# Loading two x tiles and half of the scale weights on a second DMA queue in a transformer block

## Chip, cores and metric

The kernel runs on one core of one Trainium2 chip. The metric is device time in microseconds (us), lower is better. The engines that the text names are TensorE (PE in the profile; PEld is its weight load), VectorE (DVE), ScalarE (ACT), GpSimd (POOL) and SyncE (SP). SyncE and ScalarE can both issue DMAs; each does it in its own instruction order and has its own queue (SPq and ACTq in the profile are instructions of their sequencers). The chip's 16 DMA engines move the data.

## The reference

A block with conditional layer norm (adaLN), linear attention and a gated feed-forward part, on S = 2048 rows of width D = 1024, all in bf16:

```python
mod = (silu(c) @ w_mod).reshape(...)              # sa, ca, ga, sb, cb, gb: six rows of 1024
h = layernorm(x) * (1 + ca) + sa
qkv = h @ wqkv                                     # 32 heads of 32
pq, pk = phi(q), phi(k)                            # phi(t) = where(t > 0, t + 1, exp(t)) + 1e-6
o = (pq @ (pk^T v)) / (pq . sum(pk) + 1e-6)        # per head, no softmax
x = x + ga * (o @ wo)
h = layernorm(x) * (1 + cb) + sb
x = x + gb * ((silu(h @ w_gate) * (h @ w_up)) @ w_down)   # F = 3584
```

For the change, what matters is the beginning: the scale `1 + ca` multiplies the normalized x before the first projection, so both x and the part of `w_mod` that gives `ca` (1024 x 1024) have to be on chip first.

## The kernel before

Rows are tiled by 128 (16 row tiles, "st") and by chunks of 512 (4 chunks of 4 tiles). A small planner in the file (`_Prog`) takes instructions in the order in which the code names them, puts each on its engine's list, and finds the waits from the memory that each reads and writes. It doesn't reorder: every engine, and SyncE with its DMAs, works its list from top to bottom. All instructions are recorded by one helper, so that nearly all lines of the profile have the line L176, and instructions are told apart by the names of their tiles. `P.dma` (line 192) puts a load on SyncE's list unless `queue` says otherwise. Each load has a semaphore of its own ("lane").

The work begins with the first chunk:

- Loads (lines 397 to 430): `c` (2 KB) on the ScalarE queue; then on the SyncE queue, in this order, the row tiles 0 to 3 of x (`x0_0` to `x0_3`, 256 KB each, tile XRES), `wca0` (1 MB, the first 512 columns of the scale weights, tile WCA), `wq0` (512 KB, the rows 0 to 255 of the q weights, tile WQK), `wca1` (1 MB), `wq2`, `wq4` (512 KB each), `wsa1` (1 MB, half of the shift weights), `wq6`, `wq7`, `wsa0`, then x tiles of the second chunk, the k weights, and x tiles of the third.
- TensorE transposes c, ScalarE computes silu(c) (SILUC; its function table has to be loaded first), VectorE copies it to fp32 (SILUF). TensorE fills its time with 13 dummy matmuls on a zero tile (`warm`, tiles e and ident).
- Statistics (from line 617): tile 1 on ScalarE (`act_stats`, out tile ht as a scratch), tiles 0, 2, 3 on VectorE (`bn_stats`). VectorE's order is: SILUF, statistics of tile 0, statistics of tile 2, then the factors that ScalarE needs to normalize tile 0 (`nmr`). ScalarE normalizes tiles 0 and 1, VectorE 2 and 3.
- TensorE's order then is: transposes of tile 0, 5 dummy matmuls, transposes of tile 2, `mod_sc(WCA, 8, range(2))` (16 matmuls of one column, which compute the first quarter of ca and wait for wca0), transposes of tiles 1 and 3, `mod_sc(WCA, 8, range(2, 4))`, and the first 14 matmuls of the q projection (`q_part` in `q_phase_chunk0`, line 742), which need the scaled h (`h0_first`, VectorE) and wq0. After these come `mod_sc(WCA, 8, range(4, 8))`, which waits for wca1, and the q projection with wq2, wq4 and so on.

After this start the kernel goes on through the k and q projections of all chunks, the attention products, the output projection and the feed-forward part, with TensorE at work nearly all the time.

Of the kernel before, what the change touches and what calls it, by code (L numbers as in the profile page):

```python
# [262 lines left out]
def bass_adaLN_cond__linear_attn_block__swiglu_ffn__prompt_kernel(  # L263
# [12 lines left out]
    S, D = A_x.shape[1], A_x.shape[2]  # L276
# [9 lines left out]
    with ExitStack() as es:  # L286
# [6 lines left out]
        def T(name, off, shape, dt):  # L293
            n = 1
            for s_ in shape[1:]:
                n *= s_
            assert off % 32 == 0 and off + n * mybir.dt.size(dt) <= ARENA, (name, off, shape)
            return nc.alloc_sbuf_tensor_at(name, shape, dt, offset=base + off)

        KB = 1024  # L300
        XRES = T("xres", 0, [128, NST, D], BF16)
        PQT = T("pqt", 32 * KB, [128, NHG, S], BF16)
        WCA = T("wca", 32 * KB, [128, NDT, D], BF16)
# [81 lines left out]
        xv = A_x[0].rearrange("(t p) d -> p t d", p=128)  # L385
# [6 lines left out]
        wmv = w_mod.rearrange("(kt p) n -> p kt n", p=128)  # L392
        cv8 = c.rearrange("o (kt p) -> (o kt) p", p=128)

        P = _Prog()

        P.dma("c", CS8[0:NDT, :], cv8, queue="act")
        for st in range(4):
            P.dma("x0_%d" % st, XRES[:, st, :], xv[:, st, :])

        def ca_load(p):
            P.dma("wca%d" % p, WCA[:, :, 512 * p:512 * p + 512], wmv[:, :, D + 512 * p:D + 512 * p + 512])

        def sa_load(p):
            P.dma("wsa%d" % p, WSA[:, :, 512 * p:512 * p + 512], wmv[:, :, 512 * p:512 * p + 512])
# [1 line left out]
        def wq_load(i, n=1):  # L407
            P.dma("wq%d" % i, WQK[:, i:i + n, 0:D], wqkvv[:, i:i + n, 0:D])

        ca_load(0)  # L410
        wq_load(0, 2)
        ca_load(1)
        wq_load(2, 2)
        wq_load(4, 2)
# [684 lines left out]
        for ch in range(NCH):  # L1099
# [39 lines left out]
            for j in range(4):  # L1139
                st = 4 * ch + j  # L1140
# [62 lines left out]
```

## Time and profile before

| | us |
|---|---|
| median of 3 runs (lowest to highest) | 831.15 (830.88 to 831.25) |
| the profiled execution, whole time | 831.22 |
| its span, first to last instruction | 829.4 |
| TensorE busy | 824.0 (99%) |
| VectorE busy | 312.0 (38%) |
| ScalarE busy | 197.6 (24%) |
| DMA, mean over the span | 144 GB/s |
| first transposes on TensorE (start) | 8.76 |
| first matmuls on wca0 (start) | 10.74 |
| first matmuls of the q projection (start) | 12.43 |

Times in the profile are from the start of the span. A line of the timeline gives start, duration, engine, line, operation, tiles (out<-in), shapes and count, and in square brackets the idle time before it and what ended that. For a DMA, the duration is that of its issue in the sequencer; the time from issue to landing is shown apart. A line of a wait gives who waited, for whom, the sum in us, how often, and the longest.

### The profile page before, as it was taken

The page shows a single profiled execution, that of the slowest core. Times are in us where ns is not written, and L with a number is a line of the kernel's source. Part 1 is how long each engine was busy: PE and PEld are TensorE (multiplying, and loading weights), DVE is VectorE, ACT ScalarE, POOL GpSimd, SP SyncE. Part 2 cuts the span into 40 slices and gives each one's busy share as a digit, 9 for nine tenths or more (in the row PEclk, how much of TensorE's full clock was granted, in tenths as well). Part 3 has the DMA queues.
Part 4 walks back from the last instruction along what each step waited for, and adds up shares of the span by engine and source line. Part 5 has one row for each costly group of instructions (what it writes and reads, how often), then busy time and mean ns, then how long its engine had stood idle before and what let it go on. Part 6 is the DMA issues. An engine that isn't in the chain of part 4 may idle for free.

```text
span 829.4 us, 10017 instructions
## 1 busy us (share of the span) xinstructions
PE 824.0 (99%) x4083; PEld 378.4 (46%) x4083; DVE 312.0 (38%) x665; ACT 197.6 (24%) x336; POOL 39.8 (5%) x57
## 2 busy tenths in 40 slices
PE   8999999999999999999999999999999999999998
PEld 4544444454444444444444444444444444444444
DVE  5797986756955521121221111122111111221111
ACT  4757641323242111011111101111110111111011
POOL 1010000000130000030000003000000300000000
PEclk9999999999999999999999999999999999999999
DMA  9969655928397996700455570045557004553000
GB/s 320 288 151 229 149 159 172 202 102 304 60 258 225 259 267 174 192 25 14 128 150 155 150 188 28 15 126 153 153 153 187 26 18 125 154 151 86 0 26 26
DMA packets 199245, 119.28 MB, mean 144 GB/s; under 512 B 57880, under 2 KB 182944, under 8 KB 199200
## 3 DMA queue, kind: packets, MB, share of 16 engines
q1 hardware_dynamic: 199184, 118.65, 52.7%
q8 instruction: 32, 0.52, 0.3%
q14 instruction: 13, 0.11, 0.0%
q10 hardware_dynamic: 16, 0.00, 0.0%
HBM read 100.67 MB, written 4.33 MB: 127 GB/s over the span
## 4 chain that ended last, share of the span: by engine, by line
PE 99%; DMA 1%; DVE 0%; ACT 0%; SPq 0%; issue 0%
PE ps L176 99%; DMA xres<-in_A_x_dram 1%; DVE stats L176 0%; ACT xres L176 0%; SPq L176 0%; DVE xres L176 0%; DVE mv L176 0%; DVE nmr L176 0%
## 5 line engine op out<-in xcount | busy, mean ns | idle before, releaser
L176 PE MATMUL ps<-h2t,gug 128*128 128x512 bf16 x896 | 211.7, 379 | 0.0
L176 PE MATMUL ps<-h2t,guu 128*128 128x512 bf16 x896 | 211.7, 379 | 0.0
L176 DVE TENSOR_TENSOR at<-sg,ps 128x512 bf16<-128x512 bf16 x112 | 77.1, 688 | 282.7 <-PE ps L176 281.1
L176 ACT ACTIVATE sg<-ps 128x512 bf16<-128x512 f32 x112 | 66.9, 597 | 309.7 <-PE ps L176 309.7
L176 PEld LDWEIGHTS ps<-h2t,guu 128*128 128x128 bf16 x896 | 87.5, 98 | 105.8
L176 PEld LDWEIGHTS ps<-h2t,gug 128*128 128x128 bf16 x896 | 87.4, 98 | 105.7
L176 PE MATMUL ps<-wd_a,at 128*128 128x512 bf16 (+1 forms) x512 | 112.4, 378 | 0.0
L176 PE MATMUL ps<-ht,wqk 128*128 128x512 bf16 x512 | 111.7, 379 | 0.0
L176 PE MATMUL ps<-wd_b,at 128*128 128x512 bf16 (+1 forms) x384 | 85.0, 378 | 0.0
L176 PEld LDWEIGHTS ps<-wd_a,at 128*128 128x128 bf16 x512 | 50.0, 98 | 59.8
L176 DVE TENSOR_TENSOR ut<-att,gb_b 128x512 bf16<-128x512 bf16 (+1 forms) x32 | 13.8, 430 | 167.5 <-ACT att L176 167.5
L176 PEld LDWEIGHTS ps<-ht,wqk 128*128 128x128 bf16 x512 | 49.4, 98 | 58.8
L176 ACT ACTIVATE att<-ps 128x512 bf16<-128x512 f32 (+1 forms) x32 | 17.4, 591 | 182.1 <-PE ps L176 182.1
L176 PEld LDWEIGHTS ps<-wd_b,at 128*128 128x128 bf16 x384 | 37.5, 98 | 44.7
L176 PE MATMUL ps<-pk,xres 128*128 128x512 bf16 x256 | 56.5, 379 | 0.0
L176 PE MATMUL ps<-mw,pqt 128*128 128x512 bf16 x256 | 56.3, 379 | 0.0
L176 POOL TENSOR_SCALAR h2t<-h2t,modcol 128x512 bf16<-128x512 bf16 x32 | 26.4, 841 | 383.0 <-DMA h2t<-xn 383.0
L176 ACT ACTIVATE e<-ps 128x512 bf16<-128x512 f32 x56 | 33.1, 603 | 31.7 <-PE ps L176 20.5
L176 PEld LDWEIGHTS ps<-mw,pqt 128*128 128x128 bf16 x256 | 24.8, 98 | 30.3 <-DVE xres L176 0.4
L176 PEld LDWEIGHTS ps<-pk,xres 128*128 128x128 bf16 x256 | 24.8, 98 | 30.0 <-issue 0.4
L176 ACT ACTIVATE junk<-xres 128x1024 bf16<-128x1024 bf16 x24 | 25.4, 1058 | 35.1 <-DVE xres L176 34.9
L176 DVE SCALAR_TENSOR_TENSOR xres<-ps,xres 128x512 bf16<-128x512 f32 x32 | 21.4, 689 | 12.3 <-PE ps L176 11.7
(107 smaller groups left out, 346.0 us busy)
## 6 DMA issues: line engine op xcount, KB each, us to landing
gug<-in_B_w_gate_dram SPq DMA_DIRECT2D x56, 512.0 KB, 3.9
guu<-in_B_w_up_dram SPq DMA_DIRECT2D x56, 512.0 KB, 5.2
xres<-in_A_x_dram SPq DMA_DIRECT2D x20, 256.0 KB, 7.8
rb<-recip_den SPq DMA_DIRECT2D x8, 512.0 KB, 11.5
stgx<-in_w_mod_dram SPq DMA_DIRECT2D x2, 2048.0 KB, 7.8
wd_a<-in_B_w_down_dram SPq DMA_DIRECT2D x4, 1024.0 KB, 7.8
out_dram<-xres SPq DMA_DIRECT2D x31, 128.0 KB, 1.7
xres<-in_A_x_dram SPq DMA_DIRECT2D x3, 1024.0 KB, 14.0
```

Source lines behind the costliest of these rows:

```text
L176: return getattr(e, method)(**kw)
```

## The change

The row tiles 1 and 3 of the first chunk are issued on the ScalarE queue instead of the SyncE queue, and so is the first half of the scale weights. On ScalarE's list these three issues stand behind the load of c and ahead of the load of the function table for silu(c). On SyncE's list the order becomes x0_0, x0_2, wq0, wca1, wq2, and so on as before. The lists of TensorE, VectorE and GpSimd are the same.

```diff
         P.dma("c", CS8[0:NDT, :], cv8, queue="act")
         for st in range(4):
-            P.dma("x0_%d" % st, XRES[:, st, :], xv[:, st, :])
+            P.dma("x0_%d" % st, XRES[:, st, :], xv[:, st, :], queue="act" if st % 2 else "sp")
 
         def ca_load(p):
-            P.dma("wca%d" % p, WCA[:, :, 512 * p:512 * p + 512], wmv[:, :, D + 512 * p:D + 512 * p + 512])
+            P.dma("wca%d" % p, WCA[:, :, 512 * p:512 * p + 512], wmv[:, :, D + 512 * p:D + 512 * p + 512],
+                  queue="act" if p == 0 else "sp")
```

## Prediction

> **What bounds the kernel now.** I read the chain that ended last first, in order of time, because it tells which wait the end hangs on.
>
> ```profile
> 1.71 4.21 DMA xres<-in_A_x_dram
> ...
> 5.94 1.29 DVE stats L176 x2
> ...
> 7.47 1.23 ACT xres L176
> ...
> 8.76 818.08 PE ps L176 x4069
> ```
>
> From 8.76 us on, TensorE alone carries the chain, for 818.08 us. What stands before it is the start: row tile 2 of x lands at 5.92, VectorE takes its statistics, ScalarE normalizes tile 0, and the first transposes run. So a microsecond is won or lost only in front of 8.76, or where TensorE is made to wait after it. The second view is the waits of TensorE over the whole span.
>
> ```profile
> PE ps L176 <- DMA cs<-in_c_dram: 2.2, 1, 2.2
> PE ps L176 <- ACT xres L176: 0.4, 1, 0.4
> PE ps L176 <- DVE e L176: 0.2, 1, 0.2
> ```
>
> All three lie before 8.8 us. After that no wait is listed, so nothing later can swallow a delay: what the start loses, the end loses. The third view is TensorE's timeline around the first use of the weights that the change moves (start, duration, instruction).
>
> ```profile
> 8.76 0.62 PE L176 MATMUL ps<-ident,xres 128*128 128x128 bf16 x8 [0.42 <-ACT xres L176]
> 9.21 1.24 PE L176 MATMUL ps<-e,ident 128*128 128x512 bf16 x5
> 10.29 0.61 PE L176 MATMUL ps<-ident,xres 128*128 128x128 bf16 x8
> 10.74 0.54 PE L176 MATMUL ps<-siluc,wca 128*128 128x1 bf16 x16
> 11.14 1.05 PE L176 MATMUL ps<-ident,xres 128*128 128x128 bf16 x16
> 12.03 0.54 PE L176 MATMUL ps<-siluc,wca 128*128 128x1 bf16 x16
> 12.43 3.18 PE L176 MATMUL ps<-ht,wqk 128*128 128x512 bf16 x14
> ```
>
> The scale matmuls at 10.74 read WCA's first half (wca0). Behind them in TensorE's order stand the other transposes and the first projection matmuls (12.43), which need the scale. When did wca0 land? The fourth view is the wca loads singly (issue time, then time from issue to landing), the first for half 0, the second for half 1.
>
> ```profile
> L176 SPq DMA_DIRECT2D wca<-in_w_mod_dram x1: 434/434/434, 2.6 to 2.6; - x1
> ...
> DMA to landing us min/median/max: 7.8/7.8/7.8
> ```
> ```profile
> L176 SPq DMA_DIRECT2D wca<-in_w_mod_dram x1: 479/479/479, 3.8 to 3.8; - x1
> ...
> DMA to landing us min/median/max: 11.0/11.0/11.0
> ```
>
> Half 0, issued at 2.65, landed at 10.4, only 0.3 us before its use at 10.74. Half 1, issued at 3.80, landed at 14.8. The same view of the other loads gives x tiles at 3.6, 4.2, 5.9 and 6.6, wq0 (issued 3.12, 8.7 later) at 11.8, and wq2 (4.32, 11.8 later) at 16.1. They land in the order of issue, with 1 MB of x by 6.6, 2 MB by 10.4, 2.5 MB by 11.8, 3.5 MB by 14.8, 4 MB by 16.1. The last view, of stretches of 3 us, says why (last two columns: DMA share, GB/s).
>
> ```profile
> 1.80:4.80 3.00, 2.38 (x7) 0.91 (x8) 1.92 (x8) 1.59 (x3) 0.00 (x0) 1.00 0.90 274
> 4.80:7.80 3.00, 3.00 (x9) 0.97 (x7) 2.29 (x9) 2.11 (x5) 0.57 (x1) 1.00 1.01 348
> 7.80:10.80 3.00, 2.58 (x26) 1.44 (x25) 2.83 (x8) 1.90 (x2) 1.26 (x2) 1.00 1.08 380
> 10.80:13.80 3.00, 3.00 (x57) 2.29 (x55) 2.28 (x7) 1.79 (x3) 0.00 (x0) 1.00 1.09 362
> ```
>
> The DMA engines are full from 1.8 us on. The issue of a 256 KB tile takes 0.40 to 0.43 us on SyncE, far less than the 0.7 us that 256 KB takes at 360 GB/s. The start is short of DMA bandwidth, not of issue time.
>
> **What the Trainium skill says.** "DMA: Bandwidth & Descriptors", section "Issuing engines are not separate DMA queues": DMAs from different engines end up on the same 16 DMA engines and interleave, so a second issuer saves only sequencer time. The trace of before has only one tiny load on the ScalarE queue (2 KB, c), so it can't show the interleaving, but the full DMA share fits the rest. Same page, "Queues, rings and completion order": each DMA engine goes round between the queue rows that have work, one packet at a time. No run so far shows that; it is what I build on. "ScalarE activation tables: per-element evaluation and per-set limits" gives a table load as 1283 ns; the first one here is 1.28 us, from 1.40, straight after the c load.
>
> **The change part by part.**
>
> (a) Order among the transfers, on the path. Before, one queue gave x0, x1, x2, x3, wca0, wq0, wca1, wq2. After, SyncE's queue holds x0, x2, wq0, wca1, wq2 and so on, ScalarE's holds x1, x3, wca0. Nothing is added or removed in bytes. But wca0 no longer stands ahead of wq0 and wca1: it shares with them. ScalarE's queue carries 1.5 MB; with equal bytes to each queue SyncE's gets 1.5 MB through as well, plus a lead, since x1 can be issued on ScalarE only behind c (0.78 to 1.36) where x0 goes at 0.79: 0.57 us at 274 GB/s is 0.15 MB. So wca0 ends with 3.15 MB through in place of 2 MB. In the landings of before 2.5 MB stand at 11.8 and 3.5 MB at 14.8, so 3.15 MB is 11.8 + 0.65 x 3.0 = 13.75 us. That is 3.0 us after the use at 10.74. Bounds: if the turns are packet by packet, wca0's 1 KB rows meet wq0's 2 KB rows and lose some: SyncE gets 0.17 MB more, 3.3 MB, 14.2. Below, the bytes moved in the last view come to 0.82 + 1.04 + 1.14 = 3.0 MB by 10.8, so 3.15 MB (3.3 million bytes) are through at 10.8 + 0.3/0.362 = 11.6, landed by about 11.9. That differs by 1.8 us from the landings, which follow the slowest of the engines; if that one lags less after the change, 11.9 is right. I take 13.75 since the lag is there in the one trace. TensorE starts the scale matmuls about 0.05 after the landing: 13.8 - 10.74 = +3.06 us.
>
> (b) What else is late then. Behind wca0 the spacing on TensorE stays (10.74 to 12.43), as statistics, transposes of tile 2 and the x tiles are done by then. wq0 comes earlier (two turns after x). wca1 and wq2 keep their places at 3.5 and 4 MB, 14.8 and 16.1; their uses were at 15.45 and 16.25 and move to 18.5 and 19.3. So no second stall, and no gain. The later loads (wsa, x tiles 4 on) keep their bytes ahead of them and their landing; TensorE asks for them 3 us later.
>
> (c) ScalarE: three DMA issues now stand before its table load. One costs 0.43 (SyncE's row) to 0.58 us (c on ScalarE): 1.3 to 1.75 us. The table load goes from 1.40 to 2.7 to 3.1, silu(c) ends at 4.2 to 4.6, and VectorE's copy of it, which stands ahead of the first statistics in VectorE's order, ends at 4.4 to 4.85. The statistics of tile 0 began at 3.64, so +0.75 to +1.2; those of tile 2 waited for their data until 5.94 and could have begun at 5.38 otherwise (VectorE's timeline has the last step before them from 5.21, 0.15 long), so 0.56 of this is absorbed: +0.2 to +0.65 on the first transposes, 8.76 to about 9.1. I take +0.35. It is hidden wholly in the 3.06 of (a), since TensorE waits at the scale matmuls anyway; if wca0 comes in time, it is the whole cost.
>
> (d) Arrival of x. Tile 2 is second in its queue now, but shares with tiles 1 and 3: it ends with about 0.8 MB through, near 6.1, against 5.92. Tile 1 near 4.9, tile 3 near 6.9 against 4.2 and 6.6; ScalarE's statistics of tile 1 would start at 4.9 in place of 4.27, beside (c). At zero, under (a).
>
> (e) SyncE: three issues fewer (0.41 + 0.43 + 0.43 = 1.27 us). Its later loads are issued earlier, yet the issue of wq2 already took 3.9 us in a full queue. Zero; this is what (a) uses against wca0.
>
> Sum: +3.06 us on the profiled execution's 831.22 (span 829.4, 1.8 around it), 834.3. The median of the runs is 831.15, 0.07 lower, so 834.2.
>
> **The rivals.**
> R1, the lag goes: wca0 lands at 11.9, +1.2 us, 832.4. For it: the bytes moved. Against: the landings of before.
> R2, wca0 in time, not slower: if the engines don't share evenly, but ScalarE's short queue drains ahead (large turns), wca0 has 1.5 MB of its own and about 0.5 to 0.7 MB of the other ahead, and lands by 10.4 to 11. Then only (c) is left, +0.2 to +0.65 with tile 2 at its time of before: 831.5. It decides when wca0 lands before about 11.1 (10.74 and that 0.35). Against: SyncE's queue is never empty then. That this becomes a gain is excluded: VectorE can't begin before 4.4 and needs 1.74 us from its first statistics to those of tile 2 (3.64 to 5.38) and 2.82 from there to the transposes (5.94 to 8.76), so 8.96 at the earliest, after 8.76.
> R3, SyncE's queue is favoured: wca0 comes behind all of wca1, at 14.8 or later, up to 16: +4.1 to +5.3, 835.9.
>
> **How the numbers follow.** Forecast (landing 12.8 to 14.3) 0.60; R1 0.22; R2 0.12; R3 0.06. The range leaves R2 and R3 out: 831.8 to 835.2. What a measurement of this kernel can tell from no change is about 0.2%, 1.66 us: slower is above 832.8. Forecast and R3 are slower, and about a third of R1 (0.08): 0.74. The rest of R1 and R2, but for 0.02, are the same: 0.24. Faster by 1.66 us has no mechanism that I see, so 0.02 for what I don't see.
>
> **What would show it.** In the profile after, the chain must get a DMA of wca in it, TensorE must have a wait for wca of about 2.5 to 3 us ending near 13.8, and the first projection matmuls must start near 15.5. wq0 must land at 9 to 10.3. The table load must start at 2.7 to 3.1. The stretch from the first projection to the end must keep its length. It would be wrong if wca0 landed by 11.1, or if the chain still ran through the tile-2 statistics.

## The result: 5.6 us slower

| | before | after |
|---|---|---|
| median of 6 runs each, us (lowest to highest) | 831.07 (830.88 to 831.25) | 836.66 (835.79 to 837.82) |
| the profiled execution, us | 831.22 | 837.27 |
| its span, us | 829.4 | 835.5 |
| first transposes on TensorE (start) | 8.76 | 8.80 |
| first scale matmuls, on wca0 (start): S | 10.74 | 14.53 |
| third group of scale matmuls, on wca1 (start) | 15.45 | 21.53 |
| from the first group to the third: L | 4.71 | 7.00 |

S and L are read from the profiled execution, the medians from all. The ratio of the medians is 1.0068, with a 95% interval of 1.0055 to 1.0081. The forecast was 834.2 with a range of 831.8 to 835.2: slower, as measured, but by too little.

The chain that ended last, of the kernel after (start, duration, what):

```profile
2.30 12.18 DMA wca<-in_w_mod_dram
14.48 0.05 issue
14.53 818.38 PE ps L176 x4048
```

The tile-2 statistics are gone from the chain. wca0 is in it instead, 12.18 us from its issue to its landing at 14.48, and then TensorE to the end. The three longest of TensorE's waits over the whole span, after:

```profile
PE ps L176 <- DMA wca<-in_w_mod_dram: 3.4, 1, 3.4
PE ps L176 <- DMA cs<-in_c_dram: 2.2, 1, 2.2
PE ps L176 <- ACT xres L176: 1.4, 1, 1.4
```

The first line is new. So far this is the forecast. TensorE's timeline after, around the wait, shows what is not:

```profile
8.80 0.62 PE L176 MATMUL ps<-ident,xres 128*128 128x128 bf16 x8 [1.40 <-ACT xres L176]
...
10.55 0.62 PE L176 MATMUL ps<-ident,xres 128*128 128x128 bf16 x8
14.53 0.58 PE L176 MATMUL ps<-siluc,wca 128*128 128x1 bf16 x16 [3.35 <-DMA wca<-in_w_mod_dram]
14.97 1.87 PE L176 MATMUL ps<-ident,xres 128*128 128x128 bf16 x16
16.63 0.61 PE L176 MATMUL ps<-siluc,wca 128*128 128x1 bf16 x16
17.11 4.58 PE L176 MATMUL ps<-ht,wqk 128*128 128x512 bf16 x14
21.53 0.94 PE L176 MATMUL ps<-siluc,wca 128*128 128x1 bf16 x32
```

The scale matmuls start 3.79 us later than before. But the 16 transposes behind them take 1.87 us (1.05 before), and the 14 projection matmuls, 17.11 to 21.53, take 4.42 us where 12.43 to 15.45 were 3.02 before. The same instructions run at little over half their rate until about 20. Nothing waits there. The stretches of 2 us of the kernel after say why (the third column from the right is the granted TensorE clock):

```profile
10.00:12.00 2.00, 1.12 (x11) 0.45 (x9) 1.04 (x3) 1.24 (x1) 0.56 (x1) 1.00 1.10 349
12.00:14.00 2.00, 0.00 (x0) 0.00 (x0) 0.00 (x0) 0.00 (x0) 0.00 (x0) 0.79 1.09 367
14.00:16.00 2.00, 1.47 (x27) 1.48 (x28) 0.48 (x2) 0.00 (x0) 0.00 (x0) 0.50 1.05 379
16.00:18.00 2.00, 2.00 (x27) 1.45 (x26) 1.78 (x6) 1.10 (x2) 0.00 (x0) 0.50 1.10 352
18.00:20.00 2.00, 2.00 (x6) 0.67 (x5) 0.41 (x2) 1.41 (x2) 0.00 (x0) 0.51 1.07 368
20.00:22.00 2.00, 2.00 (x27) 1.16 (x26) 0.00 (x0) 0.00 (x0) 0.00 (x0) 1.00 1.08 358
```

While TensorE sat idle its clock was halved, and it got the full clock back only at 20. A mean of 0.79 over 12 to 14 is 0.84 us at half, so the fall was at about 13.2. The account of this execution is then whole: S + 3.79 for the wait, L + 2.29 for the clock, 6.08 us, against 6.1 us between the spans.

The mean granted clock is on record for every execution. With 3.4 us at half in 835 us it would be 0.998, with 6.8 us (13.2 to 20.0 above) 0.996. Of the six executions of the kernel after, the three with 0.998 took 835.79 to 836.33, the three with 0.996 took 837.00 to 837.82, and none kept 1.000. So the loss goes with the clock from one execution to the next, and the median of 836.66 lies between the two groups.

The Trainium skill has this in "TensorE: Matmul & The Clock Gate", Part 1 (the clock gate): TensorE's clock falls to a half after an idle window of about 3.4 us and rises again after a busy window of that length, and the windows run freely. The traces agree with the half clock and with the length: it lasts 6.8 us here, twice 3.4. They don't agree with a whole idle window: the clock fell at 13.2, 2 us after TensorE's last work at 11.2. The last section has more on this.

### The profile page after: what moved, and what is told of

The parts are those of the page before. It is cut to its first block, busy times and chain, and to the rows that moved or that the text cites. A ratio compares the mean times of both kernels' runs of the same rounds, so it can differ in the third digit from the quotient of the medians.

```text
span 835.5 us, 10017 instructions
## 1 busy us (share of the span) xinstructions
PE 825.7 (99%) x4083; PEld 380.1 (45%) x4083; DVE 312.3 (37%) x665; ACT 197.6 (24%) x336; POOL 39.9 (5%) x57
## 4 chain that ended last, share of the span: by engine, by line
PE 98%; DMA 1%; ACTq 0%; DVE 0%; issue 0%
PE ps L176 98%; DMA wca<-in_w_mod_dram 1%; ACTq L176 0%; DVE xres L176 0%
```

## The experiments

**My theory** after the result: wca0's packets take turns with the other queue's, which makes it late and TensorE wait; and the idle time costs the clock, so that the time is S (wait) plus L (clock). **Rival A**: the three DMA issues on ScalarE, ahead of its table load, delay the start. **Rival B**: the clock is a by-product, and the whole loss is the wait for data. **Rival C**: two queues at once move less than one.

In every row S, L and the span are of one profiled execution, and medians and ratios are of all executions of the run; S and L are read from TensorE's timeline as above, and "sum" is (S - 10.74) + (L - 4.71). The span difference is against 829.4. In e2, e3 and e6 the clock was low ahead of S already, so there S too holds a part of the clock's cost. In e10 the sum leaves 0.3 us open; a wait of 0.2 us on VectorE elsewhere is listed there and not before.

| run | S | L | sum | span difference | median, us | before, same chip | ratio (95% interval) |
|---|---|---|---|---|---|---|---|
| e1_x_only | 11.07 | 4.75 | 0.37 | 0.4 | 832.03 | 831.53 | 1.0011 (1.0003 to 1.0020) |
| e2_wca_only | 14.58 | 5.22 | 4.35 | 4.4 | 834.28 | 831.53 | 1.0024 (1.0013 to 1.0035) |
| e3_after_fill | 16.01 | 4.72 | 5.28 | 5.3 | 835.35 | 831.53 | 1.0047 (1.0032 to 1.0062) |
| e4_one_queue_late | 15.06 | 7.58 | 7.19 | 7.2 | 837.83 | 831.53 | 1.0075 (1.0060 to 1.0090) |
| e5_late_fill | 14.80 | 4.73 | 4.08 | 4.1 | 834.43 | 831.22 | 1.0040 (1.0025 to 1.0055) |
| e6_no_warm | 12.22 | 5.09 | 1.86 | 1.9 | 832.83 | 831.22 | 1.0020 (1.0011 to 1.0028) |
| e7_wq_act | 11.29 | 4.76 | 0.60 | 0.6 | 831.98 | 831.22 | 1.0009 (1.0002 to 1.0016) |
| e8_wca_split | 11.47 | 4.73 | 0.75 | 0.7 | 832.00 | 831.22 | 1.0008 (0.9999 to 1.0017) |
| e9_after_fill2 | 14.33 | 4.73 | 3.61 | 3.6 | 834.93 | 831.37 | 1.0050 (1.0036 to 1.0063) |
| e10_sp_2k | 15.21 | 7.24 | 7.00 | 7.3 | 838.45 | 831.37 | 1.0082 (1.0069 to 1.0095) |
| e11_after | 13.70 | 7.57 | 5.82 | 5.9 | 836.89 | 831.37 | 1.0061 (1.0048 to 1.0074) |

### Which part of the change does it

**e1**, wca0 put back on SyncE's queue:

```diff
-            P.dma("wca%d" % p, WCA[...], wmv[...],
-                  queue="act" if p == 0 else "sp")
+            P.dma("wca%d" % p, WCA[...], wmv[...])
```

> Only the two x tiles go on the ScalarE queue; wca0 is back on the SyncE queue. Theory (wca0's place among the packets makes TensorE wait about 3.8 us, and the wait lets the clock fall to half for a while, about 2.3 us more): wca0 lands at 10.4 to 10.8, no wait for it over 0.3 us, clock 1.0 throughout, 831.1 to 831.6 us. Rival A (the issues on ScalarE, ahead of its table load, delay the start): two of the three issues stay, so most of the loss stays, 834 us or more.

832.03, 0.5 us over the kernel before and 0.4 over the top of my range. wca0 landed at 8.9, earlier than I had said, and L is 4.75: no clock lost in the profiled execution. Two of the three issues on ScalarE stayed, and nearly all of the loss was gone, so rival A falls. Two of the twelve executions did lose the clock (mean 0.998) and took 834.42 and 834.53. The 0.4 us of the profiled execution are the x tiles: tile 3 landed at 8.2 (6.6 before), its statistics on VectorE began at 8.27 (7.88), and tile 2, which VectorE normalizes behind them, was transposed from 10.61 (10.29).

**e2**, wca0 alone on ScalarE's queue:

```diff
-            P.dma("x0_%d" % st, XRES[:, st, :], xv[:, st, :], queue="act" if st % 2 else "sp")
+            P.dma("x0_%d" % st, XRES[:, st, :], xv[:, st, :])
```

> Only wca0 goes on the ScalarE queue; the four x tiles stay on SyncE. Theory: wca0 alternates with wq0 and wca1 and lands near 13.5 to 14.5, TensorE waits over 2.5 us for it, the clock falls, 835.5 to 837.8 us. Rival A (issues on ScalarE): one issue of the three, 831.5 to 833 us.

My theory missed here. 834.28, less than expected, and by another way. The median hides three groups: three of the eight executions kept the clock (mean 1.000) and took 832.41 to 832.56, only 1.0 us over the kernel before; four with 0.998 took 834.20 to 834.70; and the profiled one, with 0.996, was the slowest, 835.58. The kernel is the same in all three. In the profiled execution wca0, issued right behind c at 1.40, landed at 10.3, in good time. What came late were the x tiles 2 and 3, at 7.9 and 9.1. TensorE's longest wait in e2 is the normalized tile, not wca:

```profile
PE ps L176 <- ACT xres L176: 3.6, 1, 3.6
```

and the DMA queues between 4 and 5 us (q1 is SyncE's, q10 ScalarE's; packets, MB, share of 16 engines) show who had the engines:

```profile
q10 hardware_dynamic: 255, 0.26, 77.2%
q1 hardware_dynamic: 23, 0.05, 14.1%
```

The rule is the same (what stands at the head of the second queue competes with what is urgent in the first), the victim another. The idle time cost the clock here too: the 5 dummy matmuls behind the first transposes took 2.34 us, against 1.24 before.

**e7**, wq0 on ScalarE's queue in place of wca0:

```diff
-                  queue="act" if p == 0 else "sp")
+                  )
...
-            P.dma("wq%d" % i, WQK[:, i:i + n, 0:D], wqkvv[:, i:i + n, 0:D])
+            P.dma("wq%d" % i, WQK[:, i:i + n, 0:D], wqkvv[:, i:i + n, 0:D], queue="act" if i == 0 else "sp")
```

> As the changed kernel, but wq0 goes on the ScalarE queue in place of wca0 (x1, x3 and wq0 there; x0, x2, wca0, wca1 on SyncE). Three loads of the same kind on ScalarE, and the table load as late as in the changed kernel. Theory (what counts is which transfer shares with which): wca0 shares only with x3 and wq0's 16 packets for each engine, and lands by about 10.3 to 11, wq0 ahead of that; no long wait, clock 1.0, 831.6 to 832.5 us. Rival A (the issues on ScalarE): as the changed kernel, 836 us.

831.98, +0.8 us. wca0 landed at 10.3, and wq0 at 10.6, not ahead of it as I had expected. Three issues stand ahead of ScalarE's table load, which starts at 2.81 (2.79 in the changed kernel), and the loss is a seventh of the changed kernel's. This is the second time that rival A falls: it is not that there are two queues, but what is on the second.

**e8**, wca0 cut in two, one half on each queue (wca1 is cut too, with both halves on SyncE's; `...` stands for the columns):

```diff
+            for i, qu in enumerate(("act", "sp") if p == 0 else ("sp", "sp")):
+                P.dma("wca%d_%d" % (p, i), WCA[:, 4 * i:4 * i + 4, ...], wmv[:, 4 * i:4 * i + 4, ...], queue=qu)
```

> As the changed kernel, but wca0 is cut in two halves of 512 KB (k tiles 0 to 3 on ScalarE's queue, 4 to 7 on SyncE's, both behind the x tiles); wca1 is cut the same way on SyncE. Theory: both queues carry the same urgent order, so wca0 lands after 2 MB, near 10, no long wait, 831.3 to 832.2 us. Rival C (two queues at once cost throughput): wca0 lands over 1 us later than in the kernel before, 833 us or more.

832.00, +0.8 us, with an interval that includes no change. SyncE's half landed at 7.8, but ScalarE's, behind x1 and x3, only at 11.4. I had expected wca0 near 10, so this was a miss in the detail, and 1.0 us behind the 10.4 of before it stands at the bound that rival C had for the landing. But the rival's 833 us wasn't reached, and wca1 and wq2, with the same bytes ahead of them, landed earlier than before (13.6 and 14.9 against 14.8 and 16.1). In the kernel after, wq2 landed at 15.6. Two queues don't move less, so rival C falls.

### Is it the second queue, or only the order

**e4**, every load on SyncE's queue, wca0 behind wq0 and wca1 (against the kernel before):

```diff
-        ca_load(0)
         wq_load(0, 2)
         ca_load(1)
+        ca_load(0)
```

> All loads on SyncE's queue as before, only the order changed to x tiles, wq0, wca1, wca0. Theory: wca0 lands at about 14.8, where wca1 landed before, a wait near 4.1 us and the fall of the clock, 837 to 838 us. Rival A (issues on ScalarE) and rival C (two queues at once cost DMA throughput): nothing is on the second queue, so 831.1 us plus the wait alone at most, 835.2 us.

837.83, +6.3 us, with nothing on the second queue but c. wca0 landed at 15.0. TensorE's timeline in e4:

```profile
15.06 0.59 PE L176 MATMUL ps<-siluc,wca 128*128 128x1 bf16 x16 [4.38 <-DMA wca<-in_w_mod_dram]
15.50 1.87 PE L176 MATMUL ps<-ident,xres 128*128 128x128 bf16 x16
```

The same wait, the same slow transposes as in the changed kernel. So a wrong order on one queue costs what the second queue cost, and more. Rivals A and C both said 835.2 at most.

### The wait and the clock apart

**e3**, the changed kernel with dummy matmuls where TensorE waits:

```diff
+        warm(15, bank=3)
         mod_sc(WCA, 8, range(2))
```

> The changed kernel with 15 more dummy matmuls of 128x512 (15 x 0.216 = 3.2 us) ahead of the first scale matmuls, where TensorE waits for wca0. Theory: wca0 still lands near 14.5 and the scale matmuls start near 14.5, but the clock stays at 1.0 and the spacing from there to the first projection matmuls is 1.7 us as before, so 834.7 to 835.1 us. Rival B (the whole 5.6 us is the wait for data, the clock is a by-product): no change from the changed kernel, 836.7 us.

835.35, a little over the 834.7 to 835.1 expected. Three of the four executions kept the clock (mean 1.000) and took 835.12 to 835.53, as the theory says. The profiled one (0.998, 836.46, the longest of four) shows another loss. TensorE's timeline in e3:

```profile
9.12 0.97 PE L176 MATMUL ps<-ident,xres 128*128 128x128 bf16 x8 [1.97 <-ACT xres L176]
9.89 2.34 PE L176 MATMUL ps<-e,ident 128*128 128x512 bf16 x5
12.02 0.91 PE L176 MATMUL ps<-ident,xres 128*128 128x128 bf16 x8
12.77 3.18 PE L176 MATMUL ps<-e,ident 128*128 128x512 bf16 x14
16.01 0.54 PE L176 MATMUL ps<-siluc,wca 128*128 128x1 bf16 x16
```

TensorE idled for 1.97 us ahead of the first transposes, the clock fell at about 9.2, and the 5 old dummy matmuls took 2.34 us instead of 1.24. The 15 new ones (one record is missing) ran at the full rate again, but began so late that the scale matmuls came at 16.01, 2 us after wca0 had landed at 14.0. e5 and e9 are the cleaner tests.

**e5**, the same 15 dummy matmuls in e4:

```diff
+        warm(15, bank=3)
         mod_sc(WCA, 8, range(2))
```

> The one-queue kernel with wca0 late (x tiles, wq0, wca1, wca0), plus 15 dummy matmuls ahead of the first scale matmuls, so that TensorE idles only about 1.2 us there. Theory (wait plus clock): wca0 still lands at about 15.0 and the scale matmuls start there, 4.3 us later than in the kernel before, but the clock stays at 1.0: 4.3 to 4.5 us over the kernel before, some 2 us under the same kernel without the dummy matmuls (837.8), about 835.8 us. Rival B (the clock is a by-product): no change against 837.8 us.

834.43 (834.13 to 835.29), against 837.83 (837.46 to 838.39) without the dummy matmuls: no overlap. The two ran on different chips; over the kernel before on its own chip they are +3.2 and +6.3 us. The median is under the 835.8 expected; the profiled execution, 835.29, is the slowest of its four. TensorE's timeline in e5:

```profile
10.47 3.40 PE L176 MATMUL ps<-e,ident 128*128 128x512 bf16 x15
14.80 0.55 PE L176 MATMUL ps<-siluc,wca 128*128 128x1 bf16 x16 [0.93 <-DMA wca<-in_w_mod_dram]
15.21 1.05 PE L176 MATMUL ps<-ident,xres 128*128 128x128 bf16 x16
16.11 0.54 PE L176 MATMUL ps<-siluc,wca 128*128 128x1 bf16 x16
16.51 3.18 PE L176 MATMUL ps<-ht,wqk 128*128 128x512 bf16 x14
```

Useless work in the gap, data as late as in e4 (14.80 against 15.06), and the transposes are back at 1.05 us, L at 4.73. The clock's share in e4 is 7.58 - 4.73 = 2.85 us. Rival B falls.

**e6**, the kernel before without its 13 first dummy matmuls, no load moved:

```diff
-        warm(13, bank=3)
         act_stats(1)
```

> The kernel before, without its 13 dummy matmuls at the start: no load is moved, the data come at the same times. It measures the price of a half clock by itself. Theory: TensorE is at half clock from its first transposes at 8.8 for 3.4 to 6.8 us, and loses half of that time less what it would have waited for data anyway, 1.5 to 3 us: 832.8 to 834.5 us. Rival B: 831.3 us, no change, since every load is as before.

832.83, +1.6 us. Data were on time (wca0 at 10.4, wq0 at 11.8, as before), and still S is 12.22. TensorE's timeline in e6:

```profile
8.40 1.03 PE L176 MATMUL ps<-ident,xres 128*128 128x128 bf16 x8 [5.36 <-ACT xres L176]
9.23 2.34 PE L176 MATMUL ps<-e,ident 128*128 128x512 bf16 x5
11.36 1.06 PE L176 MATMUL ps<-ident,xres 128*128 128x128 bf16 x8
```

5 dummy matmuls take 2.34 us, not 1.24. That is the half clock alone, with no transfer in it.

**e9** and **e11**, on one chip: the changed kernel with 18 dummy matmuls at the start and 14 in the gap, and the changed kernel itself.

```diff
-        warm(13, bank=3)
+        warm(18, bank=3)
...
+        warm(14, bank=3)
         mod_sc(WCA, 8, range(2))
```

> The changed kernel with 18 dummy matmuls at the start in place of 13, and 14 more ahead of the first scale matmuls: TensorE has no long idle stretch up to the landing of wca0. Theory (wait plus clock): the clock stays at 1.0 from the first transposes on, wca0 still lands near 14 to 14.5, and the kernel is 3.2 to 4.1 us over the kernel before, about 2 us under the changed kernel of the same call. Rival B (the clock is a by-product): the same time as the changed kernel, 5.2 to 5.8 us over the kernel before.

> The changed kernel itself once more, on the chip of the other two runs of this call, for comparison: 5.2 to 5.8 us over the kernel before by every theory.

834.93 against 836.89: 1.96 us between the medians. TensorE's timeline in e9:

```profile
10.99 3.19 PE L176 MATMUL ps<-e,ident 128*128 128x512 bf16 x14
14.33 0.55 PE L176 MATMUL ps<-siluc,wca 128*128 128x1 bf16 x16 [0.15 <-DMA wca<-in_w_mod_dram]
14.74 1.05 PE L176 MATMUL ps<-ident,xres 128*128 128x128 bf16 x16
```

and in e11:

```profile
13.70 0.59 PE L176 MATMUL ps<-siluc,wca 128*128 128x1 bf16 x16 [2.44 <-DMA wca<-in_w_mod_dram]
14.15 1.87 PE L176 MATMUL ps<-ident,xres 128*128 128x128 bf16 x16
```

e9's data came 0.63 us later than e11's and its span is still 2.3 us shorter. The single executions overlap: one of six in each lies where the others of the other kernel do. Their mean clocks explain the one in e9: five kept 1.000 and took 834.79 to 835.83, the sixth has 0.998 and took 837.68. In e11 all six lost the clock (0.998 or 0.996); that one of them took 834.38 all the same stays open, as it has no trace. Even the kernel before lost the clock once here: ten of its eleven executions on this chip kept 1.000 and took 830.82 to 831.97, and one with 0.998 took 833.35.

### How the two queues share

**e10**, the changed kernel with SyncE's 2 KB rows (all wq loads) ahead of its 1 KB rows (wca1):

```diff
         wq_load(0, 2)
-        ca_load(1)
         wq_load(2, 2)
         wq_load(4, 2)
-        sa_load(1)
         wq_load(6)
         wq_load(7)
+        ca_load(1)
+        sa_load(1)
         sa_load(0)
```

> The changed kernel with another order behind x0 and x2 on SyncE's queue: all five wq loads (rows of 2 KB) ahead of wca1 (rows of 1 KB). wca0's own queue is not touched. If the queues alternate packet by packet, 64 of wca0's 80 turns now stand against 2 KB in place of 1 KB: 0.79 MB more go through ahead of its end, some 2.2 us at 360 GB/s, so wca0 lands at 16.2 to 16.9 and the kernel is 7.3 to 8.5 us over the kernel before. If they share by bytes, wca0 lands where it does in the changed kernel, 14 to 14.5, and the time is that of the changed kernel.

838.45, +7.1 us, just under the range. wca0 landed at 15.2 (13.65 in e11 on the same chip), not at 16.2 to 16.9: later by 1.5 us, under the 2.2 us expected, but not the zero of sharing by bytes. The DMA queues settle it. The kernel after, 9 to 11 us, where both queues hold 1 KB rows (packets, MB, share):

```profile
q10 hardware_dynamic: 356, 0.36, 55.6%
q1 hardware_dynamic: 352, 0.36, 54.6%
```

and e10 at the same time, with 2 KB rows in SyncE's queue:

```profile
q1 hardware_dynamic: 264, 0.51, 67.6%
q10 hardware_dynamic: 261, 0.27, 38.1%
```

Equal packets, twice the bytes. The queues take equal turns by packets, a packet being a row here, as the Trainium skill's "DMA: Bandwidth & Descriptors", section "Queues, rings and completion order", says of turns between queue rows. It expects several descriptors in a turn. These counts don't show how many rows a turn has, but the packets' start times in e10's trace fit one: SyncE's packets take 84 ns and ScalarE's 46, and where one ends and another starts, the next is of the other queue in about 93 of 100 cases (an estimate, since the trace doesn't say which of the 16 engines took a packet).

## Why the prediction was wrong

Point by point, by its own steps:

- **(a), wca0 late: right, the size a little under.** It was to land at 13.75, at 14.2 if the turns went by packets. It landed at 14.48 in the profiled execution, 13.65 in e11 and 14.29 in e9. The +3.06 on the scale matmuls was +3.79, +2.96 and +3.59. Packets were the better of the two rules (e10), and I took bytes. The 0.15 MB of SyncE's lead was too small: the first x packets on ScalarE's queue came only after 3.4 us, though x1 was issued at 1.42. In the kernel after, from 1.8 to 3.4 us:

```profile
q1 hardware_dynamic: 241, 0.46, 95.9%
q10 hardware_dynamic: 5, 0.00, 0.2%
```

- **(b), "Behind wca0 the spacing on TensorE stays (10.74 to 12.43)": this is the step that failed.** The spacing grew from 1.69 to 2.58 us, and the one to the third group of scale matmuls from 3.02 to 4.42. The wait of 3.4 us on TensorE wasn't only its own length; what came after it ran at half clock until 20. The prediction put this term at nothing for a reason that looks at the data alone (tiles and statistics done by then). The term is +2.29 us (2.86 in e11, 2.85 between e4 and e5). With it, 831.22 + 3.06 + 2.29 is 836.6; the other 0.7 us to the profiled 837.27 is the size of (a). The prediction had named a check that finds this: the stretch from the first projection matmuls to the end was to keep its length, and it went from 817.0 (12.43 to 829.4) to 818.4 us (17.11 to 835.5). The trace of before had a sign of it that I passed over: the 13 dummy matmuls before 8.3 us are there for something, and their weight loads lie 0.43 us apart where later ones lie 0.22.
- **(b), no second stall: right.** wca1 landed at 14.3, wq2 at 15.6, all ahead of their new uses; TensorE's list of waits has nothing after wca0.
- **(c), ScalarE: the start right, its cost too high, and hidden.** The table load started at 2.79 (2.7 to 3.1), VectorE's copy began at 4.29 and the first statistics at 4.37 (4.4 to 4.85). The first transposes came at 8.80, +0.04 where I had +0.35 (0.2 to 0.65). R2's bound of 8.96 for them was wrong too.
- **(d), x: half right.** Tile 2 landed at 4.3, not 6.1, since nothing of ScalarE's queue stood beside it; tile 3 at 8.2, not 6.9. It cost nothing here. In e1, e7 and e8, where no long wait for wca0 hides it, the transposes of tile 2 came 0.3 to 0.6 us later than before (10.61, 10.84 and 10.72, against 10.29); the other 0.3 us of e8 is wca0's late half, which landed at 11.42 just ahead of S.
- **(e), SyncE: right, at no cost.** wq0 landed at 8.6, a little earlier than the 9 to 10.3 given.
- **The rivals.** R1 (the lag goes) and R2 (wca0 in time) didn't come. R3's time, 835.9, came near the measured one by luck: it was all wait, with wca0 at 14.8 to 16, and wca0 was hardly behind wca1 (14.48 against 14.26).

No version here was measured faster than the kernel before. It feeds its first 4 MB in the order of use, and each load that I moved made something late.

## What to carry to other kernels

A second DMA queue isn't more bandwidth when the DMA engines are full already; it is another order, and it takes half of the turns away from what is urgent. Ask of each load what it will share turns with and when TensorE needs it. And price a wait of TensorE as the wait plus the clock that it may cost; the runs here show this near the start only. Useless matmuls in the gap take the second part back (e4 to e5, about 3 us).

## What I had not expected of the hardware

- The clock doesn't follow the length of a wait. Ahead of the first transposes TensorE idled for 1.97 us in e3 and 1.98 us in e7; the clock fell in e3 and stayed in e7. Freely running windows, as Part 1 of the Trainium skill's "TensorE: Matmul & The Clock Gate" has them, fit this. In stretches of 1 us the half clock lasts 6.8 us in the kernel after, e2, e4, e10 and e11, and 3.4 us in e3: two windows or one. In the 3.41 us that end at the fall, TensorE was busy for 1.39 us in the kernel after, 1.37 in e2, 1.45 in e3, 1.09 in e11, and hardly or not at all in e10 and e4. In e7 and e8 the clock came up at 5.25 and 5.81, where the trace's clock records begin; in the 3.41 us from there TensorE was busy for 1.63 and 1.66 us, and the clock stayed. So a window need not be idle throughout: in these traces the line lies between 1.45 and 1.63 us of work in 3.41.
- The granted clock in the stretches reads 1.00 from the start of the span also in e6, where the matmuls around 9 to 11 us plainly run at half rate (2.34 us for 5). The clock records of e6's trace begin only at 13.4 (at 8.2 in the kernel before), and what lies ahead of them is shown as 1.00. There I would trust the spacing of equal matmuls over that column.
- In the first microseconds the queues don't take even turns: SyncE's had nearly all from 1.8 to 3.4 in the kernel after, ScalarE's nearly all from 4 to 5 in e2. What decides it stays open.
